# Storing the m1 + m2 result beside the third product, and splitting ten left operands beside the first GEMM

## The chip, the cores and the metric

The kernel runs on one core of a Trainium2 chip. The metric is the device time of one execution in microseconds (us); three executions of the kernel before gave 489.94, 490.47 and 490.82 us, with a median of 490.47. One execution was profiled: its time was 489.94 us and its span, from the first to the last instruction, 488.2 us. The 1.74 us between the two lie outside the span.

## The reference, cut to what matters

The reference is one transformer block with adaptive layer norms on a sequence of 2048 rows of 512: linear attention first, then a dense layer to 1792 columns, Mish, and a dense layer back to 512, all in float32.

```python
x = x + ga * _A_ref(h, A_wqkv, A_wo)                 # linear attention, 32 heads
h = _layernorm(x, axis=-1) * (1 + cb) + sb
h = jnp.einsum("bsd,df->bsf", h, w1) + b1            # first GEMM of the MLP
act = h * jnp.tanh(softplus(h))                      # Mish
x = x + gb * jnp.einsum("bsf,fd->bsd", act, w2)      # second GEMM
```

The output is 2048 x 512. Every matmul operand is split into a high and a low part (`h` and `l` in the names), and a product takes three matmuls: high-high, low-high, high-low.

## The kernel before, in words

The sequence is cut into four chunks of 512 rows. Attention and the MLP of chunks 0 and 1 come first. The change touches the MLP of chunks 2 and 3 (`L = 2` and the next), which is the end of the program.

**The Strassen-like second GEMM.** For the last two chunks the second GEMM is not done block by block. The activations are called `ua` (chunk 2) and `ub` (chunk 3); a pair `g` is two neighbouring tiles of 128 hidden columns, and there are seven pairs, taken in the order 5, 6, 0, 1, 2, 3, 4. Seven products are summed over the seven pairs: m1 and m2 (run inside the loop over the pairs of the first GEMM, with a last piece after it), and then `m4`, `m6`, `m5`, `m7` and `m3`, one after the other, in the loop over `units[:4 * G]` with the counter `k` (k = 0 to 6 is m4, 7 to 13 m6, 14 to 20 m5, 21 to 27 m7) and a last loop for m3. m4 to m7 give two PSUM banks each, transposed, `banks[name][0]` and `[1]`; m3 gives four half banks, not transposed.

**Left operands.** `left_sums(g)` makes from a pair's four activation tiles the sums that products m5, m7, m6 and m3 need and notes them in `sums_of[g]`; `left_prep(name, g)` splits one of them: ACT copies the high part (line 84), DVE subtracts it for the low part (line 90). There are 35 such splits. Before the change, those of m4 for the first five pairs and four of m6 run beside the first GEMM, the rest in the loop over `k`, mostly one per unit.

**Results.** `finish(name)` is spawned when a product is complete. After m2 it forms `Q0 = m1 + m2` (two tiles), after m6 `U` and `W1`, after m5 and m7 the rest. A result tile is turned by a DVE transpose of 32 x 32 squares (`turned`), added to a tile `rq[n, c, i]` that holds the residual (`add_r`), and stored. The index n is the chunk (0 is chunk 2, 1 is chunk 3), c the half of the output columns, i one of two tiles of the half. `load_r(n, c)` loads the two tiles of a half from a DRAM copy of the residual by four transfers each, in SP's queue, and `store(n, c, i, queue)` stores one by four transfers of 64 KB. The half (0, 1) takes another way: it goes to a scratch tensor `sd` in DRAM by eight transfers of ACT's queue, is read back in rows by two transfers of SP (`rows`), and gets the four half banks of m3 added and is stored last, 128 KB at a time.

**What sets the order.** There is no automatic reordering: each engine runs its instructions in the order in which the program records them. Small pieces of work are generators: `spawn` hands one to the loop, `tick` advances each by a step, and `spawn_idle` queues one behind others, of which the first three (`width[0] = 3` at the end) advance at a tick. All SBUF tiles come from 101 slots; a tile waits for the last reader of the slot's previous tile. Transfers issued from SP and from ACT count their landing on eight counters, `DMAHW0` to `DMAHW7`, which are given out in turn in the program's order whichever of the two queues issues; before an issue, its queue waits until the previous transfer on that counter has landed. A queue issues in order, so whatever stands behind a waiting transfer waits too.

In the kernel before, `settle(Q0, 0)` (turn, add and store the half (0, 0)) is spawned at k = 25 and its stores go to ACT's queue; `settle(W1, 1)` (turn and add, no store) at k = 17.

Of the kernel before, what the change touches and what calls it, by code (L numbers as in the profile page):

```python
# [27 lines left out]
def block_kernel(ctx: ExitStack, tc: tile.TileContext, x, wqkv, wo, w1, b1t, w2, c, wmodt, out):  # L28
# [26 lines left out]
    def spawn_idle(gen):  # L55

        idle_work.append(gen)
# [1295 lines left out]
            dve.tensor_tensor(d, u, v, op=op)  # L1353
        sums_of[g] = {"m5": a22, "m7": a21, "m6": a11, "m3": a12}

    left, sums_of, early_m6 = {}, {}, []

    def left_trail(g):
        yield
# [8 lines left out]
    def turned(name, i, v):  # L1368
        t = sb(f"{name}_{i}")
        dve.transpose(t, v)  # L1370
        return t

    def add_r(n, c, i, v):
        dve.tensor_tensor(rq[n, c, i], rq[n, c, i], v, op=ALU.add)
# [31 lines left out]
    def settle(v, n):  # L1406

        for i in range(2):
            add_r(n, 0, i, turned(f"S{n}", i, v[i]))
            if n == 0:  # L1410
                store(0, 0, i, act)
            yield

    wt, SUM = {}, {"m5": 0, "m6": 1, "m7": 2, "m4": 3}
# [15 lines left out]
    for n, g in enumerate(pairs):  # L1430
        if n < 5:
            if n:
                load_rows(n)
            if n:
                load_wb(pairs[n + 1])
        if n == 5:
            load_wb(pairs[6])
        if n == 6:
            for m in pairs[:4]:
                early_m6.append(left_prep("m6", m))  # L1440
                spawn_idle(early_m6[-1])
            for m in pairs[:5]:
                load_wt("m4", m)
        def gap(c, m):
            def unit():
                e_unit(c, m)
            return unit

        if n in (3, 5):
            spawn_idle(w2_sums(SUMS_KEPT[n // 2 - 1]))  # L1450
        if n == 0:
            spawn_idle(w2_sums(2))
            begun = [pair_begin(L, pairs[i], ("tp" if i else "h", "acc")) for i in range(2)]
            tick()
        elif n == 1:
            two_pairs(L, pairs[0], g, begun, (gap(0, 0), gap(0, 1)))
            for i in range(2):
                spawn_idle(left_trail(pairs[i]))
        else:
            pair_unit(L, g, n % 2, (gap(1, 0), gap(1, 1)) if n == 2 else (gap(0, n - 1), gap(1, n - 1)))  # L1460
            if n < EARLY:
                spawn_idle(left_trail(g))

    names = ["m4", "m6", "m5", "m7", "m3"]
    units = [(name, n) for name in names for n in range(G)]
    ahead_of = [u for u in units[EARLY:] if u not in units[G:G + 4]]
    loads = list(units)
    loads = loads[5:]
    tags = {"m4": "h", "m6": "acc", "m5": "acc", "m7": "h"}
    for k, (name, n) in enumerate(units[:4 * G]):  # L1470
        for _ in range(2 if k in (6, 10, 14, 18) else 1):
            if ahead_of:
                nm, m = ahead_of.pop(0)
                spawn(left_prep(nm, pairs[m]))
        for _ in range(2 if k < 3 else 1):
            if loads:
                nm, m = loads.pop(0)
                load_wt(nm, pairs[m])
        if k in (11, 14, 17, 20):
            load_r(*{11: (1, 0), 14: (0, 1), 17: (1, 1), 20: (0, 0)}[k])  # L1480
        if k == 25:
            spawn(settle(Q0, 0))
        if k == 26:
            rows01 = [sb(f"rows_{i}", F32, (P, 2, D // 2)) for i in range(2)]
            for i in range(2):
                sp.dma_start(rows01[i], sd[0][2 * P * i:2 * P * (i + 1), :].rearrange("(t p) c -> p t c", p=P))
        if k == 17:
            spawn(settle(W1, 1))
        seventh(name, tags[name], left.pop((name, pairs[n])), wt.pop((name, pairs[n])), n, G - 1)
        if n == G - 1:  # L1490
            spawn(finish(name))
        tick()
        if k == 1:
            e_unit(0, G - 1)
            e_unit(1, G - 1)
            spawn(finish("m2"))
            tick()
# [46 lines left out]
```

## Time and profile before

| | before |
|---|---|
| median of 3 executions | 490.47 us (489.94 to 490.82) |
| profiled execution, time | 489.94 us |
| profiled execution, span | 488.2 us |
| PE busy | 478.3 us (98%) |
| DVE busy | 383.9 us (79%) |
| ACT busy | 295.7 us (61%) |
| POOL busy | 148.8 us (30%) |
| mean granted TensorE clock | 0.996 |

A row of a timeline gives the start and length in us from the span's start, the engine, the source line, the operation and the tiles written and read; rows of one group are merged, with their count. ACTq and SPq are the queues in which ACT and SP issue transfers: the length of such a row is that of the issues with the waits between them, not that of the transfers. In the list of transfers, the last number is the median from issue to landing. In the table of stretches each row gives the stretch, its length, the busy time and number of instructions of each engine, the granted TensorE clock, the share of the DMA engines and what they moved.

### The profile page before, as it was taken

Reading aid. Unit: us, or ns where it says so; the run is one execution under the profiler, and the core shown is the slowest. Engines: PE = TensorE matmul, PEld = TensorE weight load, DVE = VectorE, ACT = ScalarE, POOL = GpSimd, SP = SyncE. Lnnn points to the kernel's source line nnn. Section 1 sums busy time; section 2 is a strip of 40 time slices with the busy share of each in tenths; the row PEclk is TensorE's granted clock in tenths of the full one; section 3 lists DMA queues with packets and bytes.
Section 4 is the critical chain, followed back from the end, with each engine's and each line's share of the span. In section 5 each row is a group of like instructions: output and inputs, shape, how many; then the busy total and the mean of one; then the engine's idle time right before and its main releaser. Section 6 shows DMA issues by size and latency. Waiting matters only on the chain.

```text
span 488.2 us, 7282 instructions
## 1 busy us (share of the span) xinstructions
PE 478.3 (98%) x2342; PEld 393.4 (81%) x2342; DVE 383.9 (79%) x739; ACT 295.7 (61%) x528; POOL 148.8 (30%) x248
## 2 busy tenths in 40 slices
PE   8999999999999999999999999999999999999993
PEld 7788887878878888888888888888888888888893
DVE  7989988999799699976877665899453666877981
ACT  6777686856546879738767656663175555758000
POOL 4583320000032123103432435226344410544200
PEclk9999999999999999999999999999999999999998
DMA  8805598244864417488899989989999811899967
GB/s 308 296 9 129 143 156 255 72 144 140 296 161 109 134 38 248 131 293 288 264 339 358 327 205 232 340 235 319 366 366 293 237 46 42 198 223 197 138 120 138
DMA packets 121823, 101.69 MB, mean 208 GB/s; under 512 B 65937, under 2 KB 87449, under 8 KB 121786
## 3 DMA queue, kind: packets, MB, share of 16 engines
q1 hardware_dynamic: 79944, 54.16, 38.6%
q0 software_dynamic: 29024, 45.24, 35.2%
q10 hardware_dynamic: 12818, 1.84, 2.3%
q8 instruction: 18, 0.29, 0.2%
q14 instruction: 19, 0.16, 0.1%
HBM read 64.50 MB, written 34.61 MB: 203 GB/s over the span
## 4 chain that ended last, share of the span: by engine, by line
PE 92%; DVE 4%; ACT 1%; issue 1%; POOL 0%; ACTq 0%; DVEq 0%
PE p_a L1142 20%; PE p_s L1142 8%; PE oacc L76 5%; PE oacc L77 5%; PE oacc L78 5%; PE m L76 5%; PE m L78 5%; PE m L77 5%; PE o L76 3%; PE o L78 3%; PE o L77 3%; PE pq_a L409 3%; PE pk L76 2%; PE pk L78 2%; PE pk L77 2%; PE gacc L77 2%
## 5 line engine op out<-in xcount | busy, mean ns | idle before, releaser
L207 POOL TENSOR_TENSOR rs_n<-rs_n,half 128x1 f32<-128x1 f32 x16 | 11.4, 712 | 62.1 <-DVE rs_n L202 35.5
L1147 DVE TENSOR_TENSOR cb<-p_s,u 128x512 f32<-128x512 f32 x28 | 19.2, 687 | 12.0 <-ACT u L1183 12.0
L1152 ACT ACTIVATE u<-p_a 128x512 f32<-128x512 f32 x14 | 8.4, 598 | 25.1 <-PE p_a L1142 24.9
L1177 ACT ACTIVATE u<-p_a 128x512 f32<-128x512 f32 x12 | 7.2, 598 | 27.0 <-PE p_a L1142 27.0
L1134 ACT ACTIVATE ub<-cb,b1c 128x512 f32<-128x512 f32 x28 | 20.0, 716 | 4.2 <-DVE cb L1147 4.1
L1428 POOL DMA_DIRECT2D wt_m<-w2t x20 | 14.0, 704 | 27.7 <-PE m L78 21.6
L1183 ACT ACTIVATE u<-p_a 128x512 f32<-128x512 f32 x14 | 8.3, 595 | 15.4 <-PE p_a L1142 15.4
L1147 DVE TENSOR_TENSOR c<-p_a,u 128x512 f32<-128x512 f32 x14 | 9.6, 689 | 9.1 <-PE p_a L1142 8.8
L300 ACT ACTIVATE e_k<-pk 128x512 f32<-128x512 f32 x15 | 8.9, 592 | 10.8 <-PE pk L78 10.7
L900 POOL DMA_DIRECT2D rden_d<-rden x2 | 1.4, 720 | 45.5 <-DVE rden L898 45.5
L779 POOL DMA_DIRECT2D w2b<-w2d x20 | 10.6, 542 | 14.4 <-DVE r L1126 4.9
L84 ACT ACTIVATE l_m_4h<-u 128x512 fp32r<-128x512 f32 x2 | 1.3, 633 | 22.2 <-DMA sd<-rq 18.8
L773 POOL DMA_DIRECT2D wb<-w2d x14 | 9.9, 712 | 15.1 <-PE p_a L1142 12.2
L1111 ACT ACTIVATE u<-p_a,b1c 128x512 f32<-128x512 f32 x14 | 9.6, 686 | 5.9 <-PE p_a L1142 5.9
L303 DVE SCALAR_TENSOR_TENSOR q<-e_q,relu_q 128x512 f32<-128x512 f32 x16 | 10.7, 686 | 3.1 <-ACT relu_q L301 3.1
L303 DVE SCALAR_TENSOR_TENSOR ku<-e_k,relu_k 128x512 f32<-128x512 f32 x15 | 10.7, 713 | 3.1 <-ACT relu_k L301 3.0
L207 POOL TENSOR_TENSOR rs_x<-rs_x,half 128x1 f32<-128x1 f32 (+1 forms) x10 | 7.8, 786 | 15.8 <-DVE rs_x L202 14.6
L826 POOL DMA_DIRECT2D a1b<-rd_a x10 | 5.4, 541 | 23.3 <-PE p_a L1142 11.6
L312 POOL DMA_DIRECT2D ku<-ku x8 | 7.2, 899 | 16.5 <-DVE ku L303 16.5
L924 DVE TENSOR_TENSOR r<-o,r 128x512 f32<-128x512 f32 x16 | 10.8, 677 | 1.0 <-PE o L78 0.9
L912 DVE SCALAR_TENSOR_TENSOR q<-q,rd 128x512 f32<-128x512 f32 x16 | 10.4, 684 | 1.0 <-DMA rd<-rden_d 1.0
L929 POOL DMA_DIRECT2D x1d<-r x8 | 4.4, 549 | 20.9 <-DVE r L924 20.9
(1659 smaller groups left out, 1897.8 us busy)
## 6 DMA issues: line engine op xcount, KB each, us to landing
wm<-in_wmodt_dram SPq DMA_DIRECT2D x24, 256.0 KB, 5.5
w2b<-w2d POOLq DMA_DIRECT2D x20, 256.0 KB, 6.3
wt_m<-w2t POOLq DMA_DIRECT2D x20, 256.0 KB, 4.1
r<-in_x_dram SPq DMA_DIRECT2D x16, 256.0 KB, 4.6
x<-in_x_dram SPq DMA_DIRECT2D x15, 256.0 KB, 4.8
w1p<-in_w_dram SPq DMA_DIRECT2D x14, 256.0 KB, 4.0
w2r<-in_w_dram SPq DMA_DIRECT2D x14, 256.0 KB, 4.8
wb<-w2d POOLq DMA_DIRECT2D x14, 256.0 KB, 4.7
```

Source lines behind the costliest of these rows:

```text
L76: pe.matmul(o, st[0], mv[0], start=start, stop=False)
L77: pe.matmul(o, st[0], mv[1], start=False, stop=False)
L78: pe.matmul(o, st[1], mv[0], start=False, stop=stop)
L207: pool.tensor_tensor(y, y, half[:, lo:hi], op=ALU.pow)
L303: dve.scalar_tensor_tensor(dst, e, 1.0, r, op0=ALU.min, op1=ALU.add)
L409: pe.matmul(p, l, r, start=onto is None and c == 0 and i == 0, stop=c == 1 and i == 2, skip_group_check=onto is not None)
L779: pool.dma_start(w2s[f][i], w2d[f // 2, i][:, f % 2, :])
L924: dve.tensor_tensor(r, p, r, op=ALU.add)
L1134: act.activation(u, p, AF.Mish, bias=b1c[:, f:f + 1])
L1142: pe.matmul(p, st, mv, start=onto is None and c == 0 and i == 0, stop=c == 1 and i == 2, skip_group_check=onto is not None)
L1147: dve.tensor_tensor(out, p, u, op=ALU.add)
L1428: pool.dma_start(v, w2t[g][:, :, SUM[name], :])
```

## The change

It does four things. `settle(Q0, 0)` is spawned at k = 14 and no longer at k = 25, and its eight stores go to SP's queue. The residual halves are loaded in another order and earlier: (0, 0) at k = 8 first, then (1, 0) at 11, (0, 1) at 14 and (1, 1) at 17. Ten splits, those of m6 and of m5 for the first five pairs, are queued as idle work beside the last pair of the first GEMM; `early_prep` makes each wait until its pair's sums are recorded. And these ten are taken out of the list that the loop over `k` works off.

```diff
-    left, sums_of, early_m6 = {}, {}, []
+    left, sums_of = {}, {}
+    EARLY_SUMS = [*(('m6', m) for m in range(5)), *(('m5', m) for m in range(5))]
+
+    def early_prep(name, g):
+        while g not in sums_of:
+            yield
+        yield from left_prep(name, g)
...
             add_r(n, 0, i, turned(f"S{n}", i, v[i]))
             if n == 0:
-                store(0, 0, i, act)
+                store(0, 0, i, sp)
             yield
...
         if n == 6:
-            for m in pairs[:4]:
-                early_m6.append(left_prep("m6", m))
-                spawn_idle(early_m6[-1])
+            for nm, m in EARLY_SUMS:
+                spawn_idle(early_prep(nm, pairs[m]))
...
-    ahead_of = [u for u in units[EARLY:] if u not in units[G:G + 4]]
+    ahead_of = [u for u in units[EARLY:] if u not in EARLY_SUMS]
...
-        if k in (11, 14, 17, 20):
-            load_r(*{11: (1, 0), 14: (0, 1), 17: (1, 1), 20: (0, 0)}[k])
-        if k == 25:
+        if k in (8, 11, 14, 17):
+            load_r(*{8: (0, 0), 11: (1, 0), 14: (0, 1), 17: (1, 1)}[k])
+        if k == 14:
             spawn(settle(Q0, 0))
```

In the order below, `rq_n_c_i` is the residual tile of chunk n, half c, tile i; `x1d` the DRAM copy of the residual; `S0` the turned Q0, `S1` the turned W1, `T5` and `T7` the turned results of m5 and m7. The last number of a name is the tile's own.

SP's queue from the residual loads to the end, before:

```order
L1328 DMA rq_1_0_0_5115<-x1d_3_2452 32x16x32 x4
L1328 DMA rq_1_0_1_5120<-x1d_3_2452 32x16x32 x4
L1328 DMA rq_0_1_0_5163<-x1d_2_2301 32x16x32 x4
L1328 DMA rq_0_1_1_5168<-x1d_2_2301 32x16x32 x4
L1328 DMA rq_1_1_0_5218<-x1d_3_2452 32x16x32 x4
L1328 DMA rq_1_1_1_5223<-x1d_3_2452 32x16x32 x4
L1328 DMA rq_0_0_0_5271<-x1d_2_2301 32x16x32 x4
L1328 DMA rq_0_0_1_5276<-x1d_2_2301 32x16x32 x4
L1486 DMA rows_0_5372<-sd_5295 128x2x256
L1486 DMA rows_1_5373<-sd_5295 128x2x256
L1332 DMA out_0_dram<-rq_1_0_0_5115 32x16x32 x4
L1332 DMA out_0_dram<-rq_1_0_1_5120 32x16x32 x4
```

and with the change:

```order
L1328 DMA rq_0_0_0_5102<-x1d_2_2301 32x16x32 x4
L1328 DMA rq_0_0_1_5107<-x1d_2_2301 32x16x32 x4
L1328 DMA rq_1_0_0_5149<-x1d_3_2452 32x16x32 x4
L1328 DMA rq_1_0_1_5154<-x1d_3_2452 32x16x32 x4
L1328 DMA rq_0_1_0_5197<-x1d_2_2301 32x16x32 x4
L1328 DMA rq_0_1_1_5202<-x1d_2_2301 32x16x32 x4
L1332 DMA out_0_dram<-rq_0_0_0_5102 32x16x32 x4
L1332 DMA out_0_dram<-rq_0_0_1_5107 32x16x32 x4
L1328 DMA rq_1_1_0_5266<-x1d_3_2452 32x16x32 x4
L1328 DMA rq_1_1_1_5271<-x1d_3_2452 32x16x32 x4
L1491 DMA rows_0_5379<-sd_5314 128x2x256
L1491 DMA rows_1_5380<-sd_5314 128x2x256
```

The eight stores of (0, 0) stand between the sixth and the seventh tile's loads; the loads of (1, 1) are now behind them. The two rows of stores of `rq_1_0` and the four last stores of `rows` follow in both.

DVE from the first result of m5 to the end of the turned Q0, before:

```order
L1390 TENSOR_TENSOR U_0_4991<-m5_0_5173,U_0_4991 128x512
L1370 STREAM_TRANSPOSE T5_0_5292<-U_0_4991 128x512
L1374 TENSOR_TENSOR rq_0_1_0_5163<-rq_0_1_0_5163,T5_0_5292 128x512
L1374 TENSOR_TENSOR rq_1_1_0_5218<-rq_1_1_0_5218,T5_0_5292 128x512
L90 TENSOR_TENSOR l_m3_3l_5289<-u_2_7_4814,l_m3_3h_5288 128x512
L1390 TENSOR_TENSOR U_1_5007<-m5_1_5174,U_1_5007 128x512
L1370 STREAM_TRANSPOSE T5_1_5314<-U_1_5007 128x512
L1374 TENSOR_TENSOR rq_0_1_1_5168<-rq_0_1_1_5168,T5_1_5314 128x512
L1374 TENSOR_TENSOR rq_1_1_1_5223<-rq_1_1_1_5223,T5_1_5314 128x512
L90 TENSOR_TENSOR l_m3_4l_5323<-u_2_9_4931,l_m3_4h_5322 128x512
L1370 STREAM_TRANSPOSE S0_0_5362<-Q0_0_4992 128x512
L1374 TENSOR_TENSOR rq_0_0_0_5271<-rq_0_0_0_5271,S0_0_5362 128x512
```

and with the change, from the last of W1 on:

```order
L1394 TENSOR_TENSOR W1_1_5216<-U_1_5031,m4_1_4956 128x512
L1371 STREAM_TRANSPOSE S0_0_5225<-Q0_0_5014 128x512
L1380 TENSOR_TENSOR rq_0_0_0_5102<-rq_0_0_0_5102,S0_0_5225 128x512
L90 TENSOR_TENSOR l_m3_1l_5220<-u_2_3_4574,l_m3_1h_5219 128x512
L90 TENSOR_TENSOR l_m3_2l_5223<-u_2_5_4701,l_m3_2h_5222 128x512
L1371 STREAM_TRANSPOSE S0_1_5242<-Q0_1_5032 128x512
L1380 TENSOR_TENSOR rq_0_0_1_5107<-rq_0_0_1_5107,S0_1_5242 128x512
L90 TENSOR_TENSOR l_m3_3l_5250<-u_2_7_4814,l_m3_3h_5249 128x512
L90 TENSOR_TENSOR l_m3_4l_5262<-u_2_9_4934,l_m3_4h_5261 128x512
L1371 STREAM_TRANSPOSE S1_0_5283<-W1_0_5192 128x512
L1380 TENSOR_TENSOR rq_1_0_0_5149<-rq_1_0_0_5149,S1_0_5283 128x512
L1371 STREAM_TRANSPOSE S1_1_5292<-W1_1_5216 128x512
```

The turned Q0 has moved from behind both m5 results to ahead of them, and the last split of m3 is no longer behind the scratch stores; what follows the rows shown is the add of S1_1 and then the two m5 results as before.

ACT's last rows with what each issue waits for, before (the eight stores of `rq_0_0` stand ahead of them):

```order
L1332 DMA out_0_dram<-rq_1_1_0_5218 32x16x32 [waits DMAHW7_49,DVE_49]
L1332 DMA out_0_dram<-rq_1_1_0_5218 32x16x32 [waits DMAHW1_49]
L1332 DMA out_0_dram<-rq_1_1_0_5218 32x16x32 [waits DMAHW3_49]
L1332 DMA out_0_dram<-rq_1_1_0_5218 32x16x32 [waits DMAHW7_49]
L1332 DMA out_0_dram<-rq_1_1_1_5223 32x16x32 [waits DMAHW0_49,DVE_49]
L1332 DMA out_0_dram<-rq_1_1_1_5223 32x16x32 [waits DMAHW1_49]
L1332 DMA out_0_dram<-rq_1_1_1_5223 32x16x32 [waits DMAHW2_49]
L1332 DMA out_0_dram<-rq_1_1_1_5223 32x16x32 [waits DMAHW3_49]
```

and with the change (the eight scratch stores stand ahead of them):

```order
L1332 DMA out_0_dram<-rq_1_1_0_5266 32x16x32 [waits DMAHW1_49,DVE_49]
L1332 DMA out_0_dram<-rq_1_1_0_5266 32x16x32 [waits DMAHW3_49]
L1332 DMA out_0_dram<-rq_1_1_0_5266 32x16x32 [waits DMAHW5_49]
L1332 DMA out_0_dram<-rq_1_1_0_5266 32x16x32 [waits DMAHW7_49]
L1332 DMA out_0_dram<-rq_1_1_1_5271 32x16x32 [waits DMAHW1_49,DVE_49]
L1332 DMA out_0_dram<-rq_1_1_1_5271 32x16x32 [waits DMAHW3_49]
L1332 DMA out_0_dram<-rq_1_1_1_5271 32x16x32 [waits DMAHW5_49]
L1332 DMA out_0_dram<-rq_1_1_1_5271 32x16x32 [waits DMAHW7_49]
```

Counted out in the program's order, the previous transfer on the counter of the first `rq_1_1_1` store was, before, SP's last store of `rq_1_0_1`. With the change the fourth `rq_1_1_0` store follows SP's second load of `rows`, and the last `rq_1_1_1` store follows that fourth one.

## The prediction

> **What bounds the kernel now.** I read the chain of waits first, then the last stretches, then the two queues that issue the last stores. On the page, the busy line of PE and the chain that ended last:
>
> ```profile
> PE 478.3 (98%) x2342; PEld 393.4 (81%) x2342; DVE 383.9 (79%) x739; ACT 295.7 (61%) x528; POOL 148.8 (30%) x248
> PE 92%; DVE 4%; ACT 1%; issue 1%; POOL 0%; ACTq 0%; DVEq 0%
> ```
>
> PE sets the pace nearly everywhere, but not at the end. The stretches (busy of PE, PEld, DVE, ACT, POOL; clock, DMA share, GB/s):
>
> ```profile
> 460.00:465.00 5.00, 5.00 (x24) 4.14 (x23) 4.93 (x8) 0.00 (x0) 0.00 (x0) 1.00 0.13 22
> 465.00:470.00 5.00, 5.00 (x25) 4.14 (x24) 2.76 (x6) 0.63 (x1) 0.00 (x0) 1.00 0.57 88
> 475.00:480.00 5.00, 5.00 (x43) 4.88 (x41) 2.65 (x6) 0.00 (x0) 0.00 (x0) 1.00 0.95 141
> 480.00:485.00 5.00, 0.09 (x1) 0.00 (x0) 0.42 (x1) 0.00 (x0) 0.00 (x0) 0.94 0.84 185
> 485.00:488.20 3.20, 0.00 (x0) 0.00 (x0) 0.00 (x0) 0.00 (x0) 0.00 (x0) 0.50 0.41 62
> ```
>
> PE is full to 480.09; the last 8.1 us of the span hold one DVE add and transfers. What they are, from the timelines of ACT, SP and DVE:
>
> ```profile
> 463.29 5.25 ACTq L1396 DMA_DIRECT2D sd<-rq  x8
> 468.64 0.63 ACT L84 ACTIVATE l_m_4h<-u 128x512 fp32r<-128x512 f32 x1 [18.81 <-DMA sd<-rq]
> 471.38 14.19 ACTq L1332 DMA_DIRECT2D out_dram<-rq  x16
> 483.59 1.98 ACTq L1332 DMA_DIRECT2D out_dram<-rq  x4
> 430.38 25.95 SPq L1328 DMA_DIRECT2D rq<-x1d  x32
> 470.14 0.89 SPq L1486 DMA_DIRECT2D rows<-sd  x2
> 474.07 6.29 SPq L1332 DMA_DIRECT2D out_dram<-rq  x8
> 479.69 0.67 SPq L1332 DMA_DIRECT2D out_dram<-rq  x1
> 480.46 2.55 SPq L1511 DMA_DIRECT2D out_dram<-rows  x4
> 475.31 1.29 DVE L1374 TENSOR_TENSOR rq<-rq,T 128x512 f32<-128x512 f32 x2
> 476.52 0.75 DVE L1510 TENSOR_TENSOR rows<-rows,m 128x256 f32<-128x256 f32 x2
> 480.12 0.42 DVE L1510 TENSOR_TENSOR rows<-rows,m 128x256 f32<-128x256 f32 x1 [2.09 <-PE m L78]
> ```
>
> SP issues its last store, of the last m3 rows, by 480.46 + 2.55 = 483.01. ACT ends later, at 471.38 + 14.19 = 485.57: sixteen stores, eight of Q0 and then eight of the half (1, 1). The last four only start at 483.59, although their data was ready at 475.31 + 1.29 = 476.6, DVE's last T7 add. By the order their counter was last used by SP's store of 479.69, so they waited for its landing. That is the end of the span: a queue, not PE.
>
> ```profile
> out_dram<-rq ACTq DMA_DIRECT2D x16, 64.0 KB, 2.8
> rq<-x1d SPq DMA_DIRECT2D x32, 64.0 KB, 5.2
> y_n<-nd SPq DMA_DIRECT2D x32, 64.0 KB, 2.8
> sd<-rq ACTq DMA_DIRECT2D x8, 64.0 KB, 2.0
> out_dram<-rows SPq DMA_DIRECT2D x4, 128.0 KB, 2.5
> DMA to landing us min/median/max: 2.0/3.0/3.7
> DMA to landing us min/median/max: 2.1/2.8/9.0
> ```
>
> These are issue to landing; the last two rows are the spreads of the `out<-rq` stores and of the `y_n` loads, which have the shape of the `rq` loads. The last ACT store is issued about 0.5 us before 485.57 and lands 2.0 us later (the minimum, as it is nearly alone), at 487.1; the program ends 488.2 − 487.1 = 1.1 us after the last landing.
>
> **The change, part by part.** DVE's rows on which the new times rest, POOL's last weight loads, and two of PE's:
>
> ```profile
> 429.89 0.68 DVE L1147 TENSOR_TENSOR cb<-p_s,u 128x512 f32<-128x512 f32 x1
> 452.99 0.69 DVE L1388 TENSOR_TENSOR W<-U,m 128x512 f32<-128x512 f32 x1
> 453.59 0.68 DVE L90 TENSOR_TENSOR l_m_2l<-ub,l_m_2h 128x512 fp32r<-128x512 f32 x1
> 456.00 0.70 DVE L1370 STREAM_TRANSPOSE S<-W 128x512 f32<-128x512 f32 x1
> 456.74 0.69 DVE L1374 TENSOR_TENSOR rq<-rq,S 128x512 f32<-128x512 f32 x1
> 462.57 1.29 DVE L1374 TENSOR_TENSOR rq<-rq,T 128x512 f32<-128x512 f32 x2
> 469.91 0.71 DVE L1370 STREAM_TRANSPOSE S<-Q 128x512 f32<-128x512 f32 x1
> 472.61 0.71 DVE L1370 STREAM_TRANSPOSE T<-m 128x512 f32<-128x512 f32 x1
> 453.81 1.07 POOL L1426 DMA_DIRECT2D wt_m<-w2d  x2 [0.29 <-issue]
> 441.46 0.23 PE m L76
> 450.98 0.23 PE m L76
> ```
>
> Starts step by 0.60 us where the next operation is independent, by 0.73 where it needs the one before (456.00 to 456.74). PE's 441.46 and 450.98 are the starts of m6 and m5: 9.52 us for seven pairs, 1.36 each.
>
> *Q0 turned early.* After the second W1 (452.99) come, in the new order, transpose, add, two splits, transpose, add: the first add starts at 452.99 + 0.60 + 0.74 = 454.3 and ends at 455.0; the second starts at 456.9 and ends at 457.6. The work is moved on DVE, not added: the same two transposes and adds leave 469.91 to 472.6.
>
> *Stores to SP, loads of (1, 1) behind them.* SP's first 24 loads take three quarters of 25.95 us from 430.4, to about 450. SP then waits to 455.0, issues four stores (0.5 us each, as ACT's 1.98 for four), waits to 457.6, issues four more, to 459.7. Only then come the eight loads of (1, 1): the fourth is issued at 461.4, the eighth at 463.5. Before, they went out in the middle of the row at 430.38. Who waits: DVE's add of T5_0 to `rq_1_1_0`, at 463.2 before, and all of DVE behind it. Call X the landing of the fourth load. From the nearest rows it is 461.4 + 2.1 to 461.4 + 9.0, and 5.2 for the same loads while weights stream in (their last issues come at 453.81). The DMA engines are nearly idle at 460 to 465 (0.13), so I take 2.8 and X = 464.2, one us behind the old time. DVE then adds, finishes the second m5 tile (add, transpose, add: X + 2.8 = 467.0), and ACT issues the second scratch store to X + 4.3 = 468.5, landed 2.0 later at 470.5; SP's `rows` loads follow at 470.5 against 470.14. So this detour eats its slack and costs about nothing.
>
> POOL's order of weight loads is the same; the last is issued by 454.9, and m3, which follows m7 at 460.5 + 9.5 = 470.0, uses it 15 us later.
>
> *The last stores.* DVE no longer has Q0 between m5 and m7, so T7_0 starts when PE has finished its bank, half a pair before 470.0, at 469.4 and not at 472.61, and the second T7 add pair ends at 473.4 and not at 476.6. ACT has eight stores, from about 471.5. By the order its fourth waits for the second `rows` load to land and its eighth for that fourth. `rows` loads have no landing in the trace: they were in use at DVE's first L1510 add (476.52, without a wait), so at most 5.9 us after issue; the `y_n` median, 2.8, is the nearest from below. Landing at 471.0 + 2.8 to 5.9 = 473.8 to 476.9, the eighth ACT store goes out one store landing (3.0 to 3.7) later, 476.8 to 480.6, and lands by 479.8 to 484.3. SP meanwhile issues its eight stores of (1, 0) from 471.5, bound by the same `rows` landing, and the first three of the m3 rows as PE finishes them.
>
> *What is then last.* The fourth m3 row: PE ends at 480.09, DVE adds to 480.54, SP issues at 480.6, it lands 2.5 us later at 483.1, and 1.1 us closes the program: span **484.2 to 484.3**, against 488.2. That is 3.9 us less. With the slow ends (`rows` at 5.9, stores at 3.7) ACT's last store lands at 484.3 and the span is 485.4; if the last row's store lands in 2.0 instead of 2.5, 483.8.
>
> *Ten splits earlier.* No instruction is added. ACT's first takes the gap of 0.47 us ahead of 427.90; DVE has, from 429.89 on, three splits ahead of m4's sixth operand and one more ahead of its seventh, partly in time in which it waited before:
>
> ```profile
> 427.90 0.69 ACT L1111 ACTIVATE u<-p_a,b1c 128x512 f32<-128x512 f32 x1 [0.47 <-PE p_a L1142]
> 435.40 0.68 DVE L90 TENSOR_TENSOR l_4l<-ub,l_4h 128x512 fp32r<-128x512 f32 x1
> 437.46 0.68 DVE L1384 TENSOR_TENSOR Q<-m,U 128x512 f32<-128x512 f32 x1
> ```
>
> Counting forward in such steps, m4's last operand is ready at 437.0 (436.1 before) and PE takes it at 440.1; Q0_0, whose bank m6 takes at 442.1, is done at 439.0 (438.1 before). That leaves 3.1 us on each: costed at nothing, and one for one beyond 3.1. In return the splits of m7 and m3 come earlier, and m3's last no longer stands behind the scratch stores (the 18.81 us wait above); PE did not wait for it, so nothing is gained there.
>
> The sum against the profiled execution's own time: 489.94 − 3.9 = 486.0. That execution was the fastest of three; taken from the median, 490.47 − 3.9 = **486.6**, which I forecast.
>
> **A rule against the move to another queue.** Sixteen issues held ACT for 14.19 us, 0.89 each, but four cost only 1.98 when nothing is waited for. The Trainium skill, DMA: Bandwidth & Descriptors, section Issuing engines are not separate DMA queues, says that transfers of all issuing engines share the same 16 DMA engines, so that spreading them saves only issue time. The landings agree: 2.0 us for the scratch stores with one queue active, 3.0 for the output's with two. By that rule only the DMA work that leaves the tail counts; as an estimate, the eight scratch stores' 0.13 + 0.57 of 5 us each are 3.5 us, 0.44 a store, and eight stores fewer behind 471 would give 488.2 − 3.5 = 484.7, 487.0 for the median. It doesn't reach the sum above, which stops at PE.
>
> **The rivals.** *The rows detour sets the end.* If `rows` or the scratch stores land late, ACT's eighth store is last: it lands 3.7 + 3.7 us after the second `rows` landing. From 475.7 on this passes 483.1, and with a load of 9.0 us (480.0) the end is 487.4 + 1.1 = 488.5: no change, 490.8. For: eight more stores now run while PE is busy, at a DMA share of 0.95. Against: the row at 474.07 was issued behind the same loads, and DVE used them without a wait.
>
> *X is late, but not ruinous.* Everything from DVE's add to ACT's last store is behind X: scratch, `rows`, store, store, X + 15.4 for the last landing with the median prices above (4.3 + 2.0 + 0.6 + 2.8 + 2.8 + 2.9). It decides from X = 467.7. At the old 5.2 X is 466.6, still covered; at 9.0, 470.4, the end is 2.7 us up: 487.0, or 489.3.
>
> *Slower: SP's queue holds the loads back.* The same place, but the stores of Q0 wait for DVE and hold the (1, 1) loads longer than I reckon. Each us is paid one for one beyond X = 467.7; slower than before by over 0.2% (1 us) needs X at 472.6, the fourth load landing 11.2 us after 461.4, or the stores ready 5 us late and the load at 6.2. It would read 491.5 or more. For: DVE is full from 455 to 465 (4.93 of 5). Against: no load of this shape took over 9.0, and DVE's work ahead of the stores is counted row by row. That the change isn't made as described is excluded by the order.
>
> **How the numbers follow.** Forecast 0.74; *X late* 0.09; *rows* 0.11; *slower* 0.04; 0.02 for a gain beyond it. A measurement of this kernel tells about 0.2% (1 us) from no change. Forecast and gain beyond are faster, all of *X late* too but 0.02, and a third of *rows*: 0.87 faster, 0.09 same, 0.04 slower. The likeliest case alone spans 485.5 (0.5 less for the last landing, 0.5 for the fastest execution against the median) to 487.8 (span 485.4); with *X late* the range goes up to 489.3.
>
> **What would show it.** Right: PE ends at 480.1 in the span, the last issue is SP's fourth `out<-rows`, no issue of ACT after 480.6, the span 4 us shorter; T7_0 near 469.5; SP's eight stores near 455 to 460. Wrong: a DVE wait of several us on `rq<-x1d` after 463, `rows` issued after 473, an ACT store after 482, or a PE gap between 437 and 443.

## The result and the profile after

The changed kernel takes **487.17 us** (median of 20 executions, 485.18 to 490.96) against 489.85 us before (20 executions, 489.44 to 491.01). The ratio is 0.9946 with a 95% interval of 0.9932 to 0.9960, a gain of 2.7 us. The forecast was 486.6 us and a gain of 3.9 us.

The profiled execution took 487.04 us with a span of 485.0 us. Busy line and chain of waits on its page:

```profile
PE 477.6 (98%) x2342; PEld 393.1 (81%) x2342; DVE 384.3 (79%) x739; ACT 295.2 (61%) x528; POOL 148.4 (31%) x248
PE 91%; DVE 5%; DMA 1%; issue 1%; ACT 0%; POOL 0%; SPq 0%; DVEq 0%
```

and the stretch behind PE's end (busy of PE, PEld, DVE, ACT, POOL; clock, DMA share, GB/s):

```profile
480.00:485.00 5.00, 0.45 (x4) 0.25 (x3) 0.42 (x1) 0.00 (x0) 0.00 (x0) 0.75 0.60 148
```

The instruction counts are as before and the busy times within 0.7 us. PE ends at 480.45; before it was 480.09. The timelines of SP, ACT and DVE of the changed kernel:

```profile
455.42 5.76 SPq L1332 DMA_DIRECT2D out_dram<-rq  x8
461.27 5.12 SPq L1328 DMA_DIRECT2D rq<-x1d  x8
472.57 0.91 SPq L1491 DMA_DIRECT2D rows<-sd  x2
473.53 5.82 SPq L1332 DMA_DIRECT2D out_dram<-rq  x8
479.45 2.87 SPq L1516 DMA_DIRECT2D out_dram<-rows  x4
...
463.95 6.95 ACTq L1402 DMA_DIRECT2D sd<-rq  x8
471.82 7.63 ACTq L1332 DMA_DIRECT2D out_dram<-rq  x8
...
466.13 0.69 DVE L1380 TENSOR_TENSOR rq<-rq,T 128x512 f32<-128x512 f32 x1 [2.21 <-DMA rq<-x1d]
469.74 0.72 DVE L1371 STREAM_TRANSPOSE T<-m 128x512 f32<-128x512 f32 x1 [0.25 <-PE m L78]
480.49 0.42 DVE L1515 TENSOR_TENSOR rows<-rows,m 128x256 f32<-128x256 f32 x1 [2.10 <-PE m L78]
```

ACT is done at 471.82 + 7.63 = 479.45, where it had run to 485.57. T7_0 starts at 469.74 and not at 472.61. The last thing issued is SP's fourth row store, to 479.45 + 2.87 = 482.32, and the span ends 2.68 us later. But that issue ends 1.41 us after the last add (480.49 + 0.42 = 480.91), so PE's end alone does not set the end yet.

One measure serves for all kernels below: the **tail**, from the start of DVE's last add, which follows PE's last matmul by a few hundredths of a us, to the end of the span. Before it was 488.2 − 480.12 = 8.08 us; after it is 485.0 − 480.49 = 4.51. It takes out most of what differs between two executions ahead of PE's end, but it is read from one execution of each kernel, and three executions of the changed kernel gave 4.51, 5.19 and 4.97 us. So a difference of less than about 0.7 us between two tails says nothing by itself.

### The profile page after: what moved, and what is told of

Read it like the earlier page. It is cut to its first block, busy times and chain, and to the rows that moved or that the text cites. A ratio compares the mean times of both kernels' runs of the same rounds, so it can differ in the third digit from the quotient of the medians.

```text
span 485.0 us, 7275 instructions
## 1 busy us (share of the span) xinstructions
PE 477.6 (98%) x2342; PEld 393.1 (81%) x2342; DVE 384.3 (79%) x739; ACT 295.2 (61%) x528; POOL 148.4 (31%) x248
## 4 chain that ended last, share of the span: by engine, by line
PE 91%; DVE 5%; DMA 1%; issue 1%; ACT 0%; POOL 0%; SPq 0%; DVEq 0%
PE p_a L1142 20%; PE p_s L1142 8%; PE oacc L78 5%; PE oacc L76 5%; PE oacc L77 5%; PE m L78 5%; PE m L76 5%; PE m L77 5%; PE o L76 3%; PE o L78 3%; PE o L77 3%; PE pq_a L409 3%; PE pk L78 2%; PE pk L76 2%; PE pk L77 2%; PE gacc L77 2%
## 5 line engine op out<-in xcount | busy, mean ns | idle before, releaser
L183 DVE SCALAR_TENSOR_TENSOR wm<-wm,sc_row 128x512 f32<-128x512 f32 x16 | 10.5, 677 | 0.0
```

## The experiments

All times in us. The gain is against the kernel before on the same chip, and the ratio column is the 95% interval of the ratio; the last three columns are from each kernel's profiled execution: by how much the start of T7_0 and the issue of the rows loads lie ahead of the start of the last add (more is better), and the tail.

| kernel | median | gain | ratio | T7_0 | rows loads | tail |
|---|---|---|---|---|---|---|
| before | 489.85 | | | 7.51 | 9.98 | 8.08 |
| changed | 487.17 | 2.7 | 0.9932 to 0.9960 | 10.75 | 7.92 | 4.51 |
| changed, again | 486.81 | 3.2 | 0.9921 to 0.9948 | 10.39 | 7.22 | 5.19 |
| before, Q0's stores on SP | 490.72 | −1.0 | 1.0012 to 1.0030 | 7.52 | 6.58 | 8.70 |
| before, early splits | 486.76 | 2.9 | 0.9924 to 0.9949 | 10.75 | 10.49 | 5.25 |
| changed, splits as before | 488.40 | 1.4 | 0.9960 to 0.9982 | 8.12 | 7.81 | 5.84 |
| changed, Q0's stores on ACT | 487.64 | 2.1 | 0.9947 to 0.9977 | 9.68 | 6.51 | 6.16 |
| changed, loads first | 487.13 | 2.6 | 0.9936 to 0.9961 | 10.75 | 7.95 | 4.51 |
| changed, last store on ACT | 487.01 | 2.7 | 0.9926 to 0.9958 | 10.75 | 7.99 | 4.89 |
| changed, Q0's stores on POOL | **485.68** | 4.0 | 0.9903 to 0.9929 | 10.74 | 9.47 | 3.60 |
| before, early splits, Q0's stores on POOL | 486.68 | 3.3 | 0.9922 to 0.9947 | 10.75 | 9.89 | 4.83 |
| changed, Q0's stores on POOL, splits as before | 488.42 | 1.6 | 0.9965 to 0.9984 | 8.12 | 7.81 | 5.95 |

A profiled execution is one of several and may lie up to 1.2 us from the median of its kernel.

### Each part taken away or done alone

**The early splits undone.** In the changed kernel:

```diff
-    EARLY_SUMS = [*(('m6', m) for m in range(5)), *(('m5', m) for m in range(5))]
+    EARLY_SUMS = [('m6', m) for m in range(4)]
```

> The changed kernel, with the early splits as they were: four operands of m6 beside the first product and not ten of m6 and m5. Q0 and the loads stay as changed. Theory (the splits are covered on both sides): the time of the changed kernel, 487.2, to 0.5 us; m3's last split stands behind the scratch stores on ACT again, which may be ready 5 us later (about 471), and m3 takes it long after. Rival C (the early splits free DVE or ACT in the tail, or cost the 0.36 us by which everything stands later from 430 on): the first makes this slower by 1 us or more, 488.2; the second makes PE end 0.36 us earlier, at 480.1, and the time 486.8.

Measured: 488.40 us, 1.2 us slower than the changed kernel. The theory fell, and the first half of rival C held, including its price. From the kernel before, DVE's row of m3's last split:

```profile
469.30 0.69 DVE L90 TENSOR_TENSOR l_m_4l<-u,l_m_4h 128x512 fp32r<-128x512 f32 x1 [2.17 <-ACT l_m_4h L84]
```

and from this run's timelines of ACT and DVE:

```profile
465.83 5.25 ACTq L1402 DMA_DIRECT2D sd<-rq  x8
471.17 0.63 ACT L84 ACTIVATE l_m_4h<-u 128x512 fp32r<-128x512 f32 x1 [21.50 <-PE m L77]
...
471.83 0.69 DVE L90 TENSOR_TENSOR l_m_4l<-u,l_m_4h 128x512 fp32r<-128x512 f32 x1 [2.16 <-ACT l_m_4h L84]
472.44 0.71 DVE L1371 STREAM_TRANSPOSE T<-m 128x512 f32<-128x512 f32 x1
480.56 0.42 DVE L1515 TENSOR_TENSOR rows<-rows,m 128x256 f32<-128x256 f32 x1 [2.09 <-PE m L78]
```

and the stretch from 460 to 470:

```profile
460.00:470.00 10.00, 10.00 (x47) 8.32 (x46) 9.50 (x15) 0.00 (x0) 0.00 (x0) 1.00 0.56 87
```

m3's last split on ACT is queued behind the eight scratch stores. DVE waits 2.16 us for it, as it waited 2.17 in the kernel before, and T7 stands behind DVE: at 472.44, where it was before the change (472.61), although Q0 is long out of the way. What Q0 frees on DVE late it takes earlier: DVE is busy 9.50 of 10 us in 460 to 470 and not 4.93 + 2.76 = 7.69, and the scratch stores start at 465.83 where they started at 463.29.

**The early splits alone.** In the kernel before, only `EARLY_SUMS`, `early_prep` and the list `ahead_of` as in the change.

```diff
-            for m in pairs[:4]:
-                early_m6.append(left_prep("m6", m))
-                spawn_idle(early_m6[-1])
+            for nm, m in EARLY_SUMS:
+                spawn_idle(early_prep(nm, pairs[m]))
```

> The kernel before with one edit: the ten operands of m6 and m5 are split early. Q0 stays behind m5 on DVE and its stores on ACT, the loads as before. Prediction's step (the splits are covered, PE did not wait for m3's last one, nothing is gained): 489.9, a tail from PE's end to the end of the span of 8.1 us. New theory, from the kernel without the early splits (m3's last split stood behind the scratch stores on ACT, DVE waited 2.2 us for it, and T7 and its sixteen stores waited behind DVE, at 472.4): with the splits early DVE has nothing of m3 left at 463, so Q0 is turned at 467 to 470 and T7_0 starts at 469.4 to 469.8 and not at 472.61; ACT's sixteen stores begin at 468.6 and not 471.38, are issued by 480 to 481, and the tail shrinks by 2.5 us or more, to 5.6 or less: 486.0 to 487.4, as fast as the whole change. Rival (both are needed: early splits and early Q0, and 16 stores on ACT still run past PE): some gain, 488 to 489, ACT's last issue after 482.

Measured: 486.76 us, a gain of 2.9 us: as much as the whole change, from the part that the prediction costed at nothing. ACT and DVE:

```profile
468.41 13.56 ACTq L1332 DMA_DIRECT2D out_dram<-rq  x16
...
465.54 0.70 DVE L1371 STREAM_TRANSPOSE S<-Q 128x512 f32<-128x512 f32 x1
469.70 0.72 DVE L1371 STREAM_TRANSPOSE T<-m 128x512 f32<-128x512 f32 x1 [1.29 <-PE m L78]
480.45 0.42 DVE L1515 TENSOR_TENSOR rows<-rows,m 128x256 f32<-128x256 f32 x1 [2.10 <-PE m L78]
```

No split stands behind the scratch stores any more, so DVE turns Q0 at 465.5 to 468.4, still behind m5, and T7_0 then waits for PE and starts at 469.70. ACT's sixteen stores start at 468.41, not 471.38, and are issued by 481.97, not 485.57. The expectation had 480 to 481. ACT's is still the last issue, so the tail that is left, 5.25 us, is most likely still ACT's in this execution; SP's last landing is not on record.

**The other queue alone.** In the kernel before:

```diff
-                store(0, 0, i, act)
+                store(0, 0, i, sp)
```

> The kernel before with one edit: Q0's eight stores go out on SP, still behind the first weight products of m7 (about 471). Theory (time, then queues): ACT has eight stores in the tail and is done by about 481, but SP has 22 transfers there, its rows loads stand behind four stores of Q0 and are issued at about 473.5, and its last row stores wait for the landings of stores eight earlier, to 482 or 483; landing 2.3 and 1.1 us to the end give a span of 485.5 to 487, that is a part of the gain at most: median 487.2 to 488.8. Rival A (ACT's relief is the whole gain): the time of the changed kernel or below, 487.2. Rival B (only DMA work less in the tail counts): as the kernel before, 489.9.

Measured: 490.72 us, 1.0 us slower, which lies outside the theory and both rivals. The mechanism of the theory is there (ACT is relieved and SP's queue is late), but SP's lateness was reckoned too small: its last store was expected at 482 or 483. SP and DVE:

```profile
473.42 0.90 SPq L1486 DMA_DIRECT2D rows<-sd  x2
474.38 9.78 SPq L1332 DMA_DIRECT2D out_dram<-rq  x12
484.27 1.91 SPq L1511 DMA_DIRECT2D out_dram<-rows  x4
...
480.00 0.42 DVE L1510 TENSOR_TENSOR rows<-rows,m 128x256 f32<-128x256 f32 x1 [2.10 <-PE m L78]
```

The sixteen stores and the row stores now stand in one queue; the row stores start at 484.27, almost 4 us after the last add. ACT's relief is worth nothing by itself: the long queue has only moved from ACT to SP.

**The time alone, without the queue.** In the changed kernel:

```diff
-                store(0, 0, i, sp)
+                store(0, 0, i, act)
```

> The changed kernel, but the eight stores of Q0 go out on ACT's queue again, still early. Nothing stands ahead of SP's loads of (1, 1) any more. Theory (the gain is the time at which Q0's stores go out, and the 1.0 us that is missing from the sum comes from the loads held behind them on SP): the loads go out in the middle of one row on SP by about 457, the add of T5_0 no longer waits for them, the scratch stores come at about 463.5 and not 463.95 to 470.9, the rows loads at 470.6 to 471 and not 472.57, and the last row store follows the last add (480.5 + 0.42) at once, so the span is 484.0 to 484.3 against 485.0, and the median 486.0 to 486.4. Rival A (the gain is that ACT's queue is relieved): ACT has its 24 stores again, its last is issued after 483, and the time is that of the kernel before, 489.5 or more. Rival B (only DMA work less in the tail counts): no difference from the changed kernel, 487.2.

Measured: 487.64 us, half a us slower than the changed kernel, with intervals that overlap; neither the theory's 486.0 to 486.4 nor rival A's 489.5. By the time alone rival B (no difference) stands. The trace tells more: the tail of its profiled execution is 6.16 us. ACT, DVE and SP:

```profile
455.27 5.42 ACTq L1332 DMA_DIRECT2D out_dram<-rq  x8
460.74 0.63 ACT L84 ACTIVATE l_m_3h<-u 128x512 fp32r<-128x512 f32 x1 [11.74 <-DMA out_dram<-rq]
467.50 4.64 ACTq L1402 DMA_DIRECT2D sd<-rq  x8
...
461.40 0.69 DVE L90 TENSOR_TENSOR l_m_3l<-u,l_m_3h 128x512 fp32r<-128x512 f32 x1 [3.61 <-ACT l_m_3h L84]
...
473.83 0.95 SPq L1491 DMA_DIRECT2D rows<-sd  x2
```

Early on ACT, Q0's stores stand ahead of m3's last two splits, and DVE waits 3.61 us for one of them. All that follows is late: the scratch stores come at 467.5 and the rows loads at 473.83. So the move to SP did have a use by the trace, which the prediction did not name: it keeps stores that wait out of the queue that also splits. Its worth in time, 0.5 us, is not clear of the noise.

### What holds the last 1 us

**All loads ahead of Q0's stores.** In the changed kernel:

```diff
-        if k in (8, 11, 14, 17):
-            load_r(*{8: (0, 0), 11: (1, 0), 14: (0, 1), 17: (1, 1)}[k])
+        if k in (8, 10, 12, 13):
+            load_r(*{8: (0, 0), 10: (1, 0), 12: (0, 1), 13: (1, 1)}[k])
```

> The changed kernel, with one edit: all 32 loads of x go out ahead of Q0's stores on SP (the loads at steps 8, 10, 12 and 13 of the loop and not 8, 11, 14 and 17). Theory (the missing 1.0 us is the detour of the loads of (1, 1) behind the stores): the fourth load of (1, 1) is issued by about 453, T5_0's add no longer waits, scratch stores from 463.6, rows loads at 470.6 to 471, SP's last row store straight behind the last add at about 480.95; span 484.0 to 484.3, median 486.0 to 486.4, and the executions scatter less than the 485.2 to 491.0 of the changed kernel. Rival D (the end is set by the landing of the last store and the engines' shares, not by SP's lateness): no difference, 487.2. Rival E (two stores of Q0 now wait for landings of loads and go out later, into the weight traffic): slower than 487.2.

Measured: 487.13 us and a tail of 4.51, both as the changed kernel. SP, ACT and DVE (the adds that make the second half of the scratch data):

```profile
430.11 30.24 SPq L1328 DMA_DIRECT2D rq<-x1d  x32
460.45 6.72 SPq L1332 DMA_DIRECT2D out_dram<-rq  x8
...
463.05 6.91 ACTq L1402 DMA_DIRECT2D sd<-rq  x8
...
465.00 1.29 DVE L1380 TENSOR_TENSOR rq<-rq,T 128x512 f32<-128x512 f32 x2
```

DVE's wait for a load is gone, as expected. But the loads take until 460.35, Q0's stores come behind them at 460.45, and ACT's scratch stores take 6.91 us, because most of them wait on a counter that one of SP's stores or loads holds. With SP idle the kernel before needed 5.25, although DVE made its data 0.8 us later (465.84). So one detour is swapped for another: the rows loads come at 471.64, 0.9 us earlier, but so does PE's end, and against the last add they have gained nothing (7.95 against 7.92). Rival E's mechanism is there too: Q0's stores waited for landings and went out until 460.45 + 6.72 = 467.17. This run does not tell the theory from rival D.

**The last store on another queue.** In the changed kernel:

```diff
-        sp.dma_start(out[512 * L + P * t:512 * L + P * (t + 1), D // 2:D], v)
+        (act if t == 3 else sp).dma_start(out[512 * L + P * t:512 * L + P * (t + 1), D // 2:D], v)
```

> The changed kernel with one edit: the fourth of the last four row stores goes out on ACT, which is done with its own at 479.45, and not on SP behind three that wait for landings. Theory (SP's last store is held 1.0 us beyond the last add by the waits of the stores ahead of it): it is issued within 0.1 us of the add's end; tail from PE's end to the end of the span 3.6 to 4.0 and not 4.55 us, unless the third row store on SP, which still waits, lands last; median 486.2 to 486.7. Rival (the landing shares the DMA engines with the stores ahead and comes when they are through): tail 4.4 or more, 487.2.

Measured: 487.01 us, no gain. SP, ACT and DVE:

```profile
479.51 2.13 SPq L1516 DMA_DIRECT2D out_dram<-rows  x3
...
480.76 0.36 ACTq L1516 DMA_DIRECT2D out_dram<-rows  x1
...
480.31 0.42 DVE L1515 TENSOR_TENSOR rows<-rows,m 128x256 f32<-128x256 f32 x1 [2.10 <-PE m L78]
```

The fourth store is issued at 480.76, 0.03 us after its add, as the theory had it, but now SP's third is the last, issued to 481.64: the exception that the expectation names. The lateness is that of SP's whole queue and not of one store.

**Q0's stores on POOL.** In the changed kernel they go out behind POOL's last weight load, so that they stand ahead of nothing and take none of the counters that SP and ACT share:

```diff
-                store(0, 0, i, sp)
+                pass
...
+        if k == 27:
+            for i in range(2):
+                store(0, 0, i, pool)
```

> The changed kernel, but Q0's eight stores go out on POOL's queue, behind its last weight load (about 455 to 459). Neither SP's loads of (1, 1) nor ACT's splits stand behind them. Theory (in the changed kernel the detour of the loads makes T5_0's add wait 2.2 us and puts the rows loads at 472.57; on ACT Q0's stores hold m3's splits, and DVE waited 3.6 us for one): both waits are gone, scratch stores from 463 to 463.5, rows loads at 470 to 470.7, T7_0 at 469.4; all stores of SP and ACT 1 to 2 us earlier, tail 3.7 to 4.1 us, median 486.2 to 486.8. Rival (the tail depends on the last landings, not on when rows come): tail 4.4 to 4.6, 487.1. Rival (POOL's stores take DMA engines or landings from the scratch stores): slower than 487.5.

Measured: **485.68 us** (485.40 to 485.86), faster than both kernels: 4.0 us less than before, about the 3.9 us of the prediction's sum. The interval of its ratio lies below that of the changed kernel's first comparison and overlaps a little with that of the second. POOL, SP and DVE:

```profile
456.87 2.00 POOL L1332 DMA_DIRECT2D out_dram<-rq  x3
459.12 0.65 POOL L1332 DMA_DIRECT2D out_dram<-rq  x1 [0.26 <-DMA wt_m<-w2d]
460.32 2.57 POOL L1332 DMA_DIRECT2D out_dram<-rq  x4 [0.55 <-issue]
...
470.53 0.89 SPq L1491 DMA_DIRECT2D rows<-sd  x2
471.48 6.58 SPq L1332 DMA_DIRECT2D out_dram<-rq  x8
478.15 2.63 SPq L1519 DMA_DIRECT2D out_dram<-rows  x4
...
480.00 0.42 DVE L1518 TENSOR_TENSOR rows<-rows,m 128x256 f32<-128x256 f32 x1 [2.10 <-PE m L78]
```

The rows loads come at 470.53, where the prediction had them, and SP's last store is issued to 480.78, 0.36 us after the last add's end and not 1.41. The tail of 3.60 us and the median are a little better than the theory expected (3.7 to 4.1, 486.2 to 486.8). Rival B of the first runs, by which only the DMA work in the tail counts, falls here, since the stores go out at nearly the same stage. Whether the loads of (1, 1), the freed counters or something else in which POOL's queue differs did it, this run alone does not separate; the run with the loads first says that the loads alone are not enough.

**The floor.** The changed kernel without the sixteen stores of (1, 0) and (1, 1), so that this part of the output is missing; one execution.

```diff
                 add_r(1, 0, i, t)
-                store(1, 0, i, sp)
                 add_r(1, 1, i, t)
-                store(1, 1, i, act)
```

> The changed kernel without the sixteen stores of the halves (1, 0) and (1, 1); this part of the output is left out. It measures the floor of the tail. The prediction's sum has 0.45 us from PE's end to the add's, the store at once, 2.5 us to its landing and 1.1 us to the end: 4.1 us of tail. Theory (0.4 us of the tail of 4.55 is the queue, the rest is the floor): tail 3.4 to 4.1, landing 2.0 to 2.5 us after the issue. Rival (the floor itself is 4.5): no change.

Measured: a tail of 3.35 us. SP and DVE:

```profile
476.31 4.42 SPq L1514 DMA_DIRECT2D out_dram<-rows  x4
...
479.95 0.42 DVE L1513 TENSOR_TENSOR rows<-rows,m 128x256 f32<-128x256 f32 x1 [2.10 <-PE m L78]
```

With nothing else to store, the issue ends 0.36 us after the add and the span 2.57 us after the issue. So of the changed kernel's 4.51 us, 1.05 are SP's queue (1.41 − 0.36) and 0.11 the rest; with the stores on POOL 0.25 are left.

### The two causes crossed

**Early splits, Q0 late, its stores on POOL**, that is, the kernel with the early splits alone and the edit above:

> The kernel before with the ten early splits, and Q0's eight stores on POOL behind its last weight load; Q0 itself stays behind m5 on DVE, the loads as before. Theory (what the tail needs is that m3's last split is not behind the scratch stores and that neither SP nor ACT has Q0's stores; that Q0 is early adds nothing): rows loads at 470 to 470.5, T7_0 at 469.4 to 469.7, ACT's last issue by 478.5; from the start of the last add to the end of the span 3.4 to 3.8 us, median 485.5 to 486.0, as with early Q0 on POOL (485.68). Rival (Q0's stores, now at 467 to 471, slow the landings of the rows loads and the last stores): 4.5 us or more, 486.6 or more.

Measured: 486.68 us and a tail of 4.83, so the rival. The stretch 470 to 475, first of the changed kernel with the stores on POOL, then of this one:

```profile
470.00:475.00 5.00, 5.00 (x44) 5.00 (x43) 3.66 (x7) 0.00 (x0) 0.00 (x0) 1.00 0.74 166
```

```profile
470.00:475.00 5.00, 5.00 (x44) 5.00 (x43) 3.58 (x7) 0.00 (x0) 1.78 (x3) 1.00 0.98 208
```

and this one's timelines of POOL and SP:

```profile
466.58 5.20 POOL L1332 DMA_DIRECT2D out_dram<-rq  x8 [10.54 <-DMA sd<-rq]
...
470.89 7.99 SPq L1332 DMA_DIRECT2D out_dram<-rq  x8
```

Both have their rows loads at 470 and T7_0 at 469. But with Q0 late its stores run at 466.6 to 471.8, the DMA engines are at 0.98 and not 0.74 in 470 to 475, and SP's eight stores take 7.99 us and not 6.58. This is what an early Q0 buys, together with the earlier loads that go with it: 0.7 us by the two gains and 1.2 by the two tails. The intervals of the two ratios just overlap, so the size is not firm. The new order of the loads was not tried by itself.

**Q0 early on POOL, splits as before:**

> The changed kernel with Q0's stores on POOL, and the early splits undone (four of m6, as before). Theory (early splits and Q0's stores are two separate causes): scratch stores at about 463.5 to 464, m3's last split on ACT behind them at 469, T7_0 behind it on DVE at 470 to 470.6 and not 469.3, so 0.7 to 1.3 us of the stores' lead is lost; SP and ACT still have no store of Q0: from the last add's start to the end 3.5 to 4.5 us, median 485.7 to 486.7. Rival (the early splits are worth the same 1.2 us as with the stores on SP, or more): 486.9 or more.

Measured: 488.42 us, the rival. Its timelines of ACT and DVE:

```profile
466.91 5.25 ACTq L1402 DMA_DIRECT2D sd<-rq  x8
...
473.53 0.71 DVE L1371 STREAM_TRANSPOSE T<-m 128x512 f32<-128x512 f32 x1
481.65 0.42 DVE L1518 TENSOR_TENSOR rows<-rows,m 128x256 f32<-128x256 f32 x1 [2.10 <-PE m L78]
```

T7_0 and the rows loads lie exactly where they do with the splits as before and the stores on SP (8.12 and 7.81 ahead of the last add). In both, the splits left to DVE delay the scratch stores, which hold the rows loads, and m3's last split stands behind the scratch stores and holds T7_0. So POOL's queue brings nothing clear of the noise without the early splits (gains of 1.6 and 1.4), and by the gains these are worth 1.3 us with the stores on SP and 2.4 with the stores on POOL.

### The scatter of the changed kernel

Twice more the changed kernel itself, for its executions differ by up to 5.8 us where those of the kernel before differ by 1.6.

> The changed kernel once more, for the scatter of its executions (485.2 to 491.0, those of the kernel before 489.4 to 491.0). If the scatter is in the tail (each of SP's and ACT's stores waits for the landing of the store eight before, so a late landing is passed on through three or four of them), PE ends at 479.5 to 480.5 as in the eight profiles so far, and the time from the last add's start to the end changes by what the execution is longer or shorter than 487.0, around 4.5 us. Rival (the scatter comes from PE, which waits somewhere or runs at a lower granted clock): the tail is 4.5 us and PE's end moves by that difference.

> The changed kernel a third time, one more profile for the same question: tail changed and PE's end at 479.5 to 480.5, or tail 4.5 us and PE's end moved.

Measured: the five new executions have a median of 486.81 us, and the single one after them took 488.12. The three profiled executions have their last add at 480.49, 479.61 and 481.13 and tails of 4.51, 5.19 and 4.97 us (spans of 485.0, 484.8 and 486.1). So PE's end moves by 1.5 us and the tail by 0.7; the rival carries more of it, but not all: between the first two, PE ends 0.88 us earlier and the span only 0.2, because SP's queue was late in both (its last issue ended at 482.32 and 482.20). The waits of PE (total, times, longest) in the first of these executions:

```profile
PE tp_x L543 <- ACT x L216: 1.0, 1, 1.0
```

and in the third; the second has neither:

```profile
PE tp_x L543 <- ACT x L216: 1.1, 1, 1.1
...
PE o L78 <- DVE qs_2l L90: 0.4, 1, 0.4
```

Waits of 1.0 and of 1.1 + 0.4 us in parts of the program that the change does not touch fit the 0.9 and 1.5 us by which PE ends later than in the second. One DVE row far ahead of the change shows that the difference is there early: the split `a_13l` starts at 300.22, 299.34 and 300.87 in the three, and at 299.86 in the kernel before. No profile caught an execution of 488.5 to 491 us, so what makes those is open, and so is why the kernel before shows less of it. The record has one hint: the mean granted TensorE clock was 0.993 and 0.995 in the two longest executions (490.96 and 488.83 us) and 0.997 to 1.000 in the others. In the three traces the clock is 1.00 in every stretch up to 480 us and lower only behind, so a low mean would fit a long tail; this is not shown.

## Why the prediction was right, and where not

**What bounds the kernel: right.** The end was a queue of stores and not PE; in the kernel before it was ACT's. With the sixteen stores of (1, 0) and (1, 1) left out of the changed kernel, the tail falls to the floor of 3.35 us. To relieve ACT alone was no gain, since SP's queue was then last.

**Q0 turned early, stores on SP: right in kind, reckoned 1.5 us too early.** The stores were issued at 455.42 to 461.18 (reckoned 455.0 to 459.7); the loads behind them at 461.27 (459.8); X, the landing that T5_0's add waits for, came at 466.1 and not 464.2. Of each difference 0.37 us is that of this execution as a whole (below); most of the rest of the first two is the issue of the eight stores, which took 5.76 us and not 4.7.

**"This detour eats its slack and costs about nothing": wrong, and the mis-sized term of the sum.** X stayed below the 467.7 from which the prediction charged it, and yet it cost. By the prediction's own chain (X + 4.3 for the last scratch store, 2.0 for its landing) the 1.9 us went whole into the rows loads: 466.1 + 4.3 + 2.0 = 472.4, and they went out at 472.57, not 470.5. SP's stores wait for the landing of these loads and of each other, and the last one was issued 1.05 us later than the floor allows. The prediction followed this lateness along ACT's stores alone, up to X + 15.4, and took SP's row stores as free. With Q0's stores on POOL, rows loads and last store come when the sum has them, and the gain is 4.0 us, if also by two errors that offset each other in part (the landing and the time outside the span, next).

**The landing of the last store: too long.** The sum had 2.5 + 1.1 us from the issue, about 3.2 from its end; it was 2.68. This gave back 0.5 us of the 1.05.

**Two terms that the sum did not have.** The last add came 0.37 us later than in the execution before; executions of the changed kernel differ by 1.5 us there, and the DVE row `a_13l`, far ahead of the change, already starts 0.36 us later (300.22 against 299.86), so this is not of the change. And 2.04 us lay outside the span and not 1.74. So 486.0 for that execution became 486.0 + 0.37 + 0.38 + 0.30 = 487.04, where 0.38 is the tail (4.51 against 484.25 − 480.12 = 4.13). The median of three that the prediction started from, 490.47, lay 0.6 us above that of twenty, which is why 486.6 looks closer than the gain was.

**The ten splits "costed at nothing" and "nothing is gained there": the second wrong.** The cost was right: PE has no gap at 437 to 443 (busy 10.00 of 10 us from 435 to 445). The gain was not. The prediction saw that m3's last split stood behind the scratch stores and asked only whether PE waited for it. DVE did (2.17 us in the kernel before, 2.16 in the run with the splits as before), with T7 and sixteen stores behind it. It booked T7_0's 3.2 us on Q0 leaving DVE ("DVE no longer has Q0 between m5 and m7, so T7_0 starts … at 469.4"). Without the early splits T7_0 is at 472.44 with Q0 moved; with them it is at 469.70 with Q0 not moved. The sum came out near the mark because the change holds both parts; for either part alone it would have failed: the splits alone bring 2.9 us, the rest without them 1.4. As far as the account of the 3.2 us goes, the hit was luck.

**The rule against the other queue.** The prediction set beside its sum that, by the Trainium skill, DMA: Bandwidth & Descriptors, section Issuing engines are not separate DMA queues, all issuing engines share the same 16 DMA engines and spreading saves only issue time; it gave 487.0. The time came out there, but the runs don't bear out the reason. With the same eight stores issued at nearly the same stage the kernel took 487.64 us from ACT, 487.17 from SP and 485.68 from POOL. ACT and SP are not told apart by these times; POOL's interval lies clear of SP's first comparison and overlaps a little with its second. What differs in the traces is which work stands behind the stores in a queue that keeps its order: a split for which DVE waits 3.61 us on ACT, loads for which it waits 2.21 us on SP. The part of the rule on shared engines fits another pair of runs: with eight stores at 467 to 472 and not 457 to 463, eight others take 7.99 us and not 6.58.

**The rivals.** *X is late* and *rows* were both at work in small, as lateness of SP's queue, and neither came to set the end in the form priced. *Slower: SP's queue holds the loads back* did not happen: the loads went out 1.5 us later than reckoned, and X came at 466.1 where this rival needed 472.6.

**The signs.** Of those for being right, the last issue is SP's fourth row store, no issue of ACT comes after 480.6, and T7_0 starts at 469.74; the span is 3.2 us shorter and not 4. Of those for being wrong, one was partly there from the start: DVE waited 2.21 us on `rq<-x1d` at 466.13. In the third profiled execution, with its last add 0.64 us later, that wait was 2.64 us and the rows loads went out at 473.66, behind the 473 of the second sign. They pointed at the detour on SP, which did cost.

## What to carry to other kernels

When a stall is taken away, ask of every engine behind it, and not only of the busiest one, what it waited for; a wait that costs the bottleneck nothing can hold the results that are stored last. In a tail of stores, count per queue: what waits in it, what stands behind, and which counters it shares with other queues; put transfers that can wait into a queue with nothing behind them. And test the parts of a change apart, since here the part that was costed at nothing brought as much as the whole.

## What the runs showed of the hardware

- With the same eight stores of 64 KB issued from ACT, SP or POOL the change as a whole gained 2.1, 2.7 to 3.2 and 4.0 us; ACT's and SP's gains are not told apart by the intervals. POOL issued four in 2.57 us, 0.64 each.
- Eight scratch stores on ACT, ready at about 463, took 5.25 us with SP idle and 6.91 with SP's stores among them on the shared counters, although there the data was made 0.8 us earlier.
- The time outside the span depends on the program: 1.7 to 1.9 us in the kernel before, in those made from it, and in the changed kernel with its loads first or its splits as before; 2.0 to 2.1 us in the changed kernel and its other variants. The cause is open.
